# Attention and mixture of experts on one core: every queue in a new order, and twenty filling products instead of thirty

## The chip, the cores and the metric

The kernel runs on one core of one Trainium2 chip, in one launch. The metric is the time of the launch on the device, in microseconds (us); lower is better. Of the engines of a core the kernel uses TensorE (PE in the profile; its weight loads are listed as PEld), VectorE (DVE), ScalarE (ACT), GpSimd (POOL) and SyncE (SP), which only issues transfers.

## What is computed

Eight batches, eight heads, 576 positions, head size 64. The first half computes masked attention per head: heads 0 to 3 see the last 32 positions (local), heads 4 to 7 see every 32nd position (strided). The second half feeds the 512 wide result to four experts, each a causal attention of its own, weighted by a gate that keeps two of four experts per position.

```
scores = scale * q @ k.T;  mask_local = 0 <= rel < 32;  mask_strided = rel >= 0 and same residue mod 32
x = softmax(where(mask, scores, -1e9)) @ v            # (B, S, 512)
logits = x @ w_gate;  w = softmax over the two largest of four
for e in range(4):
    qe, ke, ve = x @ wq[e], x @ wk[e], x @ wv[e]
    a = softmax(where(causal, scale * qe @ ke.T, -1e9))
    out += (e is kept) * w * (a @ ve @ wo[e])
```

## The kernel before

The whole program is written as 2655 small pieces of work ("ops"), collected in a list `OPS`: each has a kind, a batch, the engines that may run it, the buffers that it reads and writes and a function that emits its instructions. Nothing in the code that collects them sets the order. The order is written out in `PLAN`, a table of words: a word such as `63P340` means op 63, on TensorE (P; A is ScalarE, D VectorE, G GpSimd, S SyncE), and the digits behind it give the buffer of a ring that each new tile of the op takes, of eight banks of PSUM for instance. `schedule()` walks through the table and emits each op on the engine that the word names. So the table sets the order on each engine, who evicts a bank, which queue issues a load, and which bank or buffer a tile lies in.

The ops of a batch, with the lines that the profile shows: loads of q and k (L519, L522 for the first heads, L560 later) and of v (L581, L587, L594), most on SyncE, a few on ScalarE and GpSimd; transposes of q and k on TensorE (L539) for the first heads and on VectorE (L571) later; for the first two batches a product that puts the mask into the bank (L643, from `m_loc` or `m_str`); scores of the first attention (L613, L625 local, L632 strided; 72 or 44 products, each of a few rows); row maximum, subtraction, exponential, sum, reciprocal and scaling (L667 to L705; maximum and sums on VectorE, exponential on ScalarE); value products (L757, L777 local, L800 strided; 76, 84 or 44 small products); then x in two parts, `xh` and `xl` (L321, L743). From x the second half takes projections (L944 in batch 0, L933 later; 12 products of 288 columns for half a tile), values (L854, L862), scores (L1035, L987), transposes of the attention weights (L1100, into tiles `th`, evicted in L321), products with V (L1133; 12 or 20) and the output (L1168; 6 products of 512 columns).

The kind `fill` is one product of 448 columns of ones (L336) into a bank that nobody reads; there are `NF` of them, and the table says where they stand. `warm` is eight more of 328 columns at the very start.

```python
        for word in PLAN.split():
            i = 0
            while word[i].isdigit():
                i += 1
            o, slots = OPS[int(word[:i])], iter(word[i + 1:])
            for u in o.uses:
                if not u.taken:
                    u.ring.take(u, int(next(slots)))
            o.fn(ENGINE[word[i]])
    def spin(i):
        wb = RB.new(f"spin{i}")
        op("fill", "P", 448, 0, lambda e: ones(wb, 448), r=[fz], w=[wb], mode=M128)
```

Of the kernel before, what the change touches and what calls it, by code (L numbers as in the profile page):

```python
# [20 lines left out]
def attention_moe_kernel(  # L21
# [72 lines left out]
    NF = 30  # L94
    batch = [0]

    def op(kind, eng, n, key, fn, r=(), w=(), mode=None, npk=0, after=()):
# [26 lines left out]
        17G0123 56S0 4D0 14D01 0D0 10D00 5G 57S 2P01234567 95S0 16D01 3G0 6A 7A 59S 18G0 58A 21A1 92A0 22A 8A  # L124
        96S 9G 24S 15G012 2625P0 71P0 70P1 153P2 91S 23S 93S 2626P3 2627P3 2628P3 2629P3 2630P3 2631P3 2632P3
        63P340 60P56 64A 94S 109P7 65A 61D 35P3 62A 36P4 135S1 72P0 138S1 74D0 134S 73D 76D 139S 75D 78A 136S
        77A 2633P5 2634P5 2635P5 2636P5 2637P5 2638P5 2639P5 2640P5 2641P5 25P561 79D 137S 28P01 27A 26D 29A
        222S0 30D 80D 2642P6 100P650 97P01 224S 81D 102A 37P1 98D 99A 83G 221S 101D 82G 110P5 38D1 223S 111P0
        104G0 39D 41D 236P0 67S1 40D 43A 143P161 112D2 107G 140P43 69S 144A 113D 141A 142D 66S 152P1 145A 114D
        105G 68S 235P3 42A 84D0 154P1 116A 34S2 45D 225P470 115D 106G 201S0 155D3 228P65 227A 44D 226A 32S 230A  # L130
        229D 117A 118D 103G 31S 2643P7 2644P7 237P0 156D 33S 46D 119D 85P7400 47G 192S0 158D 120D 160A 157D 122G
        189S 48D 159A 121D 108G 177S1 49D1 2645P5 2646P5 2647P5 2648P5 123P560 146S1 161D 125A 50P2111 149G 162D
        124A 86A 239D0 180S 88A 163D 87D 193A0 53A 165D 126P6522 195S2 164G 51A 89D 178A0 54D 148G 198S 190A 52D
        191D0 2649P7 2650P7 2651P7 166P741 289S0 238D 1222P10 167A 90G 241D 151S 150G 131A 1260P21 194D 196A
        179D0 1216P7 181A 240D 1261P 183S3 132D 1202P0 242A 147G 182D 1253P3 293S1 127D 129A 168A 1217P 199A
        128D 1209P5 290S 243D 197G 1210P 202S 1223P 130D 12G0 184A 292S 1254P 185D 133G 1262P 338G2 208S1
        169P4633 186S 291S 1218P 174A 172D 200G 244D 203A0 287S 1255P 175D 1A 11G 173D 1211P 170D 212S 1246P6
        13D0 19D0 401S2 171D 1224P 245D 1247P 187A 209S 1248P 188G 295D1 234S0 1203P 288S 20G012345 1204P 213A
        1256P 205S 204G0 1205P 254S1 1225P 210A 214G 1207D0 1263P 286S 1266P4 55G 1264D 324S3 1212P 1226D 1219P
        206A 331S4 211D 1214A 1267P 207G 246D0 1213A 329S 1268P 1206D 397S1 1269P 1228D0 1249P 1208G 328S 1270D  # L140
        1229P50 1250A 294D 253S 176G 1257A 1215G 1251A1 233S 1220A 1258A 336G 303P0 326S 302P6 1230D 304P0 1221D
        325S 1265D1 1305P350 330S 305D1 296G1 306D 327S 1275P7200 307D 255S 1307D0 1237P6 1252G 256S 308D 1276D1
        334G 309A 402S 1280D 1231P5 1306D 337S 1271A 1277D 1308A 1281D 297G 339S 310D 1235P0 1282A 469S0 1272D
        1309A 311D 299S 333D0 312G 1238A 1233P7 1236A 1283A 232S 332D 1227A 218S2 1259G 1232A 1279A 1239P3 362S4
        1273P2401 1234A 1240A 368S3 1242D00 260P601 1241G000 1284P151 1366D2 1243A 364S 1278A 1310D 1361P731
# [1049 lines left out]
    for b in range(B):  # L1195
# [50 lines left out]
```

## Time and profile before

| | |
|---|---|
| median of 3 runs | 447.31 us (447.0 to 447.91) |
| the profiled execution | 443.71 us |
| its span, first to last instruction | 442.0 us |
| TensorE busy | 424.8 us (96%) |
| VectorE busy | 344.0 us (78%) |
| GpSimd busy | 247.8 us (56%) |
| ScalarE busy | 245.9 us (56%) |

A profile shows one execution, here one of 443.71 us. Busy times are the union of an engine's instructions. Products on TensorE overlap, several of them being in the array at once, so a product's own duration is longer than what it adds to the path; what a group adds is read from the start of the group to the start of the next, or from the chain of waits. The chain that ended last runs through TensorE for 81% of the span.

### The profile page before, as it was taken

What the parts mean: (1) busy time and instruction counts of PE and PEld (TensorE: products, weight loads), DVE (VectorE), ACT (ScalarE), POOL (GpSimd) and SP (SyncE); (2) the same over time, 40 slices, a digit from 0 to 9 for tenths busy, and PEclk for the clock granted to TensorE, in tenths of its full rate; (3) what the DMA queues carried; (4) which work ended last, traced back from release to release, by engine and by line L of the source; (5) the groups of instructions that cost most, each with busy time, mean ns of one, the idle gap of its engine ahead of it and who ended that gap; (6) DMA issues with size and microseconds to landing.
All of it is one profiled execution on the core that took longest, in us unless ns stands there. A gap on an engine that the chain in (4) does not pass through costs nothing.

```text
span 442.0 us, 18545 instructions
## 1 busy us (share of the span) xinstructions
PE 424.8 (96%) x7504; PEld 370.3 (84%) x7504; DVE 344.0 (78%) x1043; ACT 245.9 (56%) x759; POOL 247.8 (56%) x439
## 2 busy tenths in 40 slices
PE   7989998999999998999999998999999999999996
PEld 3669977898889976899888897988989998997875
DVE  1797998889999697987798768988787966464833
ACT  3544497425674676634866522852876455557640
POOL 3487776446657357365548441856468522665800
PEclk9999999999999999999999999999999999999999
DMA  8768765664466454644054654557130210003024
GB/s 169 156 138 156 146 129 112 110 111 80 73 135 137 83 94 100 122 92 90 14 104 98 124 104 85 120 114 158 27 73 10 75 49 27 1 2 120 18 82 142
DMA packets 190899, 41.76 MB, mean 94 GB/s; under 512 B 185552, under 2 KB 185808, under 8 KB 190814
## 3 DMA queue, kind: packets, MB, share of 16 engines
q1 hardware_dynamic: 187550, 39.25, 42.6%
q8 instruction: 59, 0.97, 0.9%
q0 software_dynamic: 960, 0.76, 0.8%
q10 hardware_dynamic: 2304, 0.57, 0.6%
q14 instruction: 26, 0.21, 0.2%
HBM read 31.11 MB, written 9.44 MB: 92 GB/s over the span
## 4 chain that ended last, share of the span: by engine, by line
PE 81%; DVE 6%; DMA 3%; SPq 3%; issue 3%; ACT 2%; ACTq 0%; DVEq 0%
PE bank L933 17%; PE bank L1133 10%; PE bank L1168 10%; PE bank L854 9%; PE bank L1035 6%; PE bank L1100 6%; PE bank L800 3%; PE bank L777 3%; PE bank L944 3%; PE bank L625 2%; PE bank L632 2%; PE bank L987 2%; PE bank L862 2%; DVE qkt L571 2%; PE bank L336 2%
## 5 line engine op out<-in xcount | busy, mean ns | idle before, releaser
L1081 POOL TENSOR_SCALAR p<-p,st,wt 128x128 f32<-128x128 f32 (+3 forms) x128 | 77.0, 615 | 20.5 <-DVE st L1061 11.8
L1053 ACT ACTIVATE p<-p,st 128x512 f32<-128x512 f32 (+3 forms) x128 | 72.0, 567 | 8.9 <-DVE st L1048 8.8
L1048 DVE CUSTOM_DVE_ANT_0 p<-bank,m_cau 128x512 f32<-128x512 f32 (+3 forms) x128 | 57.5, 480 | 5.3 <-PE bank L1035 4.1
L571 DVE STREAM_TRANSPOSE qkt<-nat 128x576 f32<-128x576 f32 x52 | 53.0, 1026 | 8.2 <-DMA nat<-in_k_dram 4.3
L321 ACT COPY th<-bank 128x256 f32<-128x256 f32 (+2 forms) x119 | 44.9, 437 | 12.7 <-PE bank L1100 11.9
L1133 PE MATMUL bank<-th,vs 128*64 128x192 f32 (+4 forms) x512 | 48.0, 337 | 0.0
L1133 PEld LDWEIGHTS bank<-th,vs 128*64 128x64 f32 x512 | 33.7, 137 | 14.3 <-issue 7.6
L854 PE MATMUL bank<-wh_v,xh 128*128 128x260 f32 x128 | 36.8, 287 | 0.0
L854 PE MATMUL bank<-wh_v,xl 128*128 128x260 f32 x128 | 36.2, 283 | 0.0
L854 PE MATMUL bank<-wl_v,xh 128*128 128x260 f32 x128 | 36.1, 282 | 0.0
L743 DVE TENSOR_TENSOR xl<-bank,xh 128x128 fp32r<-128x128 f32 (+4 forms) x104 | 32.0, 336 | 4.8 <-ACT xh L321 4.6
L321 ACT CAST xh<-bank 128x270 fp32r<-128x270 f32 (+4 forms) x64 | 20.0, 352 | 25.2 <-PE bank L800 12.6
L1100 PE MATMUL bank<-ident,p 64*128 64x64 f32 x800 | 33.9, 227 | 0.1
L962 POOL TENSOR_TENSOR qkl<-kf,qk 128x288 fp32r<-128x288 f32 x32 | 25.6, 805 | 14.8 <-DVE qk L321 6.2
L933 PE MATMUL bank<-xh,wh_q 128*128 128x288 f32 x112 | 33.7, 301 | 0.0
L933 PE MATMUL bank<-xh,wh_k 128*128 128x288 f32 x112 | 33.6, 300 | 0.0
L1100 PEld LDWEIGHTS bank<-ident,p 64*128 64x128 f32 x800 | 29.2, 138 | 4.7 <-issue 1.3
L933 PE MATMUL bank<-xh,wl_k 128*128 128x288 f32 x112 | 33.0, 295 | 0.0
L933 PE MATMUL bank<-xh,wl_q 128*128 128x288 f32 x112 | 33.0, 294 | 0.0
L933 PE MATMUL bank<-xl,wh_k 128*128 128x288 f32 x112 | 33.0, 294 | 0.0
L933 PE MATMUL bank<-xl,wh_q 128*128 128x288 f32 x112 | 33.0, 294 | 0.0
L705 POOL TENSOR_TENSOR p1s<-p1s,st 128x648 f32<-128x648 f32 (+1 forms) x16 | 19.3, 1209 | 21.4 <-DVE st L703 14.5
(179 smaller groups left out, 1260.0 us busy)
## 6 DMA issues: line engine op xcount, KB each, us to landing
out_dram<-ys SPq DMA_DIRECT2D x31, 256.0 KB
nat<-in_q_dram SPq DMA_DIRECT2D x104, 72.0 KB
nat<-in_k_dram SPq DMA_DIRECT2D x104, 72.0 KB
v<-in_v_dram SPq DMA_DIRECT2D x72, 40.0 KB
v<-in_v_dram SPq DMA_DIRECT2D x110, 22.5 KB
v<-in_v_dram SPq DMA_DIRECT2D x52, 27.0 KB
out_dram<-ys SPq DMA_DIRECT2D x10, 128.0 KB
v<-in_v_dram SPq DMA_DIRECT2D x24, 48.0 KB
```

What stands on the lines that cost most here:

```text
L321: (nc.scalar.copy if e == "ACT" else nc.vector.tensor_copy)(dst, src)
L571: nc.vector.transpose(dst, src)
L743: op("xl", "D", n_, key + 0.5, lambda e, s_=s_, x_=x_: nc.vector.tensor_sub(x_(xl.t), s_(xa.t), x_(f(xh.t))), r=[xa, xh[u]], w=[xl[u]])
L854: nc.tensor.matmul(vp.t[:m, :NV], xx.t[:, t0:t0 + m], ww.t[:, kt, :], start=i == 0, stop=i == 11)
L933: nc.tensor.matmul(pj.t[:, :HS], ww.t[:, kt, ep * 128:(ep + 1) * 128], xx.t[:, c], start=i == 0, stop=i == 11)
L1035: nc.tensor.matmul(sp[a].t[:, c0:c0 + nk], x.t[r, 0, q0:q0 + 128], y.t[r, 1, :nk], start=i == 0, stop=i == 2)
L1048: lambda e, sp=sp, p=p, a=a, nk=nk, ci=ci, c0=c0: nc.vector.tensor_tensor_reduce(out=p.t[:, a, :nk], in0=sp[a].t[:, c0:c0 + nk], in1=m_cau ...
L1053: op("exp2", "A", nk, k_ + 1, lambda e, p=p, a=a, ci=ci, nk=nk: nc.scalar.activation(p.t[:, a, :nk], p.t[:, a, :nk], AF.Exp, bias=st.t[:, ...
L1081: lambda e, p=p, a=a, ci=ci, t=t, nk=nk: nc.gpsimd.tensor_scalar(p.t[:, a, :nk], p.t[:, a, :nk], st.t[:, 14 + ci + a:15 + ci + a], wt.t[:, ...
L1100: nc.tensor.transpose(tp[hf].t[:, 64 * c:64 * c + 64], src, f(ident.t[r, r]))
L1133: nc.tensor.matmul(acc.t[o, c0:c0 + cn], vw, th[a].t[:, s0:s0 + cn], start=j == 0, stop=j == idx[-1], skip_group_check=True)
L1168: nc.tensor.matmul(yp.t[:, :w_], xx.t[:, c0:c0 + 128], ww.t[:, ep, c:c + w_], start=i == 0, stop=i == 5)
```

## The change

Two things differ. `NF` goes from 30 to 20, so ten filling products are gone. And the whole table `PLAN` is another one: all ops but the ten are still there, in another order, on partly other engines, in other buffers. Of the ops that may run on more than one engine, evictions of transposed attention weights stood 119 times on ScalarE and 41 times on VectorE and now stand 109 and 51 times; evictions of V 28 and 12 times, now 23 and 17; evictions and casts of x into `xh` 64 and 40 times, now 69 and 35; those of projections 40 and 24 times, now 43 and 21. On TensorE 146 semaphore instructions become 154. GpSimd issues 34 transfers of v instead of 30.

```diff
     OPS = []
-    NF = 30
+    NF = 20
...
     PLAN = """
-        17G0123 56S0 4D0 14D01 0D0 10D00 5G 57S 2P01234567 95S0 16D01 3G0 6A 7A 59S 18G0 58A 21A1 92A0 22A 8A
...
```

Its places, as the order of the instructions shows them (the names are tiles with their numbers; the rows of an engine stand in the order in which it runs them).

ScalarE at the start, before: `m_loc` is the local mask, copied three times; the four transfers are of q and k.

```order
L370 ACT_TABLE_LOAD
L370 CAST m_loc_77<-m_loc_77 32x320 x2
L519 DMA vs_105<-in_k_dram 64x9x64
L519 DMA vs_106<-in_q_dram 64x9x64
L519 DMA p_97<-in_q_dram 64x8x64
L519 DMA vs_106<-in_q_dram 64x9x64
L370 CAST m_loc_77<-m_loc_77 32x320
L321 COPY qkt_112<-bank_67 128x256
```

And now:

```order
L522 DMA ys_82<-in_q_dram 64x2x64
L332 ACT_TABLE_LOAD
L332 ACTIVATE fz_74<-fz_74 128x1
L519 DMA vs_105<-in_k_dram 64x9x64
L519 DMA vs_105<-in_q_dram 64x9x64
L370 CAST m_loc_77<-m_loc_77 32x320
L519 DMA vs_106<-in_k_dram 64x9x64
L370 CAST m_loc_77<-m_loc_77 32x320 x2
L321 COPY qkt_112<-bank_68 128x320
```

One transfer now stands ahead of the table load, two ahead of the first copy and one between the copies.

TensorE behind the first scores (L613), before: nine filling products (L336, a weight load and a product each) follow them, and then the transposes of the second pair of heads (L539 from `vs1`); two of the nine are shown.

```order
L643 MATMUL bank7_71<-m_str0_78,ident0_76 128x324
L643 MATMUL bank3_67<-m_loc0_77,ident0_76 128x320
L643 MATMUL bank4_68<-m_loc0_77,ident0_76 128x256
L613 MATMUL bank1_65<-qkt0_112 32x64 x20
L613 MATMUL bank0_64<-qkt0_112 32x64 x16
L336 LDWEIGHTS fz0_74
L336 MATMUL bank5_69<-fz0_74 128x448
L336 LDWEIGHTS fz0_74
L336 MATMUL bank5_69<-fz0_74 128x448
```

And now:

```order
L539 MATMUL bank6_70<-ident0_76,vs0_105 128x64
L539 MATMUL bank7_71<-ident0_76,vs0_105 128x64
L613 MATMUL bank3_67<-qkt0_112 32x64 x20
L613 MATMUL bank2_66<-qkt0_112 32x64 x16
L539 MATMUL bank4_68<-ident0_76,vs1_106 128x64
L539 MATMUL bank5_69<-ident0_76,vs1_106 128x64
```

The transposes of the second pair follow the first scores directly; the mask products moved ahead of the first transposes or behind these.

TensorE in the middle of the program, before, where the profile has 288 us: scores of a strided pair of heads (L632) and behind them value products of a local pair (L777, the first four of its pieces).

```order
L632 MATMUL bank4_68<-qkt1_113 64x54
L777 MATMUL bank7_71<-pt11_120,v12_116 64x64 x2
L777 MATMUL bank3_67<-pt11_120,v12_116 64x64 x2
L777 MATMUL bank2_66<-pt11_120,v12_116 64x64 x2
L777 MATMUL bank0_64<-pt11_120,v12_116 64x64 x2
```

In front of the same value products stand now (the six rows of L1168 whole, the first four of twelve of L933):

```order
L632 MATMUL bank2_66<-qkt1_113 64x54
L1168 MATMUL bank5_69<-wh_o0_169,oh2_151 128x512
L1168 MATMUL bank5_69<-wh_o0_169,ol2_154 128x512
L1168 MATMUL bank5_69<-wl_o0_170,oh2_151 128x512
L1168 MATMUL bank5_69<-wh_o0_169,oh0_149 128x512
L1168 MATMUL bank5_69<-wh_o0_169,ol0_152 128x512
L1168 MATMUL bank5_69<-wl_o0_170,oh0_149 128x512
L933 MATMUL bank7_71<-xh5_130,wh_q0_165 128x288
L933 MATMUL bank7_71<-xl5_136,wh_q0_165 128x288
L933 MATMUL bank7_71<-xh5_130,wl_q0_166 128x288
L933 MATMUL bank7_71<-xh4_129,wh_q0_165 128x288
```

Six output products (L1168) and twelve projection products (L933) now stand between the two groups of small products.

## Rows read from the trace of the kernel before

**Rows 1.** The page: busy us (share of the span), instructions.

```profile
PE 424.8 (96%) x7504; PEld 370.3 (84%) x7504; DVE 344.0 (78%) x1043; ACT 245.9 (56%) x759; POOL 247.8 (56%) x439
```

**Rows 2.** Waits of TensorE, 40 to 430 us: us in total, times, longest us.

```profile
PE bank L800 <- issue: 1.7, 1, 1.7
PE bank L777 <- issue: 1.5, 2, 1.1
PE bank L625 <- issue: 1.2, 1, 1.2
PE bank L1035 <- issue: 1.0, 1, 1.0
PE bank L757 <- issue: 0.8, 1, 0.8
PE bank L800 <- DVE st L703: 0.5, 1, 0.5
```

**Rows 3.** Windows between resumptions: length, busy us (instructions) per engine, clock, DMA share, GB/s.

```profile
171.04:244.30 73.26, 71.91 (x1396) 63.05 (x1395) 63.06 (x189) 44.33 (x136) 43.50 (x70) 1.00 0.42 84
244.30:270.10 25.80, 24.56 (x379) 22.65 (x380) 18.42 (x58) 11.12 (x37) 9.44 (x15) 1.00 0.64 122
270.10:289.80 19.70, 18.63 (x383) 16.91 (x383) 18.67 (x49) 10.44 (x34) 13.02 (x23) 1.00 0.42 89
```

**Rows 4.** DMA queues: packets, MB, share of 16 engines; q8 is TensorE's instruction queue.

```profile
q8 instruction: 59, 0.97, 0.9%
```

**Rows 5.** Timeline of TensorE: start us, us, line, count [idle before <- releaser].

```profile
166.88 1.79 PE L625 MATMUL bank<-qkt 64*32 64x64 f32 x144
...
266.61 1.55 PE L800 MATMUL bank<-pt,v 54*64 54x54 f32 x88
...
270.13 0.34 PE L625 MATMUL bank<-qkt 64*32 64x64 f32 x13 [1.24 <-issue]
```

**Rows 6.** Windows from a block's first instruction to the resumption, longest and shortest.

```profile
239.82:244.30 4.48, 3.47 (x132) 3.02 (x128) 4.14 (x13) 2.84 (x9) 4.19 (x8) 1.00 0.49 99
266.84:270.10 3.26, 2.06 (x143) 1.86 (x136) 2.43 (x13) 2.05 (x8) 0.17 (x1) 1.00 0.65 155
```

**Rows 7.** Timeline of TensorE at the start.

```profile
5.96 1.12 PE L643 MATMUL bank<-m_loc,ident 128*128 128x256 f32 x2 [1.85 <-ACT m_loc L370]
...
7.16 2.76 PE L336 MATMUL bank<-fz 128*128 128x448 bf16 x7
9.86 0.78 PE L539 MATMUL bank<-ident,vs 64*128 64x64 f32 x18
...
12.53 1.90 PE L336 MATMUL bank<-fz 128*128 128x448 bf16 x9
...
32.82 0.40 PE L944 MATMUL bank<-xh,wh_q 128*128 128x288 f32 x1
```

**Rows 8.** Windows at the start; columns as in rows 3 (third count: VectorE).

```profile
0.00:10.00 10.00, 6.78 (x23) 3.06 (x25) 1.49 (x8) 2.65 (x4) 3.79 (x22) 1.00 0.85 167
10.00:40.00 30.00, 27.48 (x728) 22.18 (x727) 24.95 (x66) 15.91 (x43) 19.39 (x33) 1.00 0.72 150
```

**Rows 9.** The chain of waits in order of time: start us, us, what.

```profile
77.42 1.45 PE bank L1133 x12
...
291.30 1.58 PE bank L933 x12
292.88 1.41 PE bank L1168 x6
```

**Rows 10.** Timeline of ScalarE, its third copy of the mask.

```profile
5.37 0.46 ACT L370 CAST m_loc<-m_loc 32x320 fp32r<-32x320 f32 x1 [2.07 <-DMA vs<-in_q_dram]
```

**Rows 11.** Timeline of GpSimd, ten issues of loads of v.

```profile
18.25 6.33 POOL L594 DMA_DIRECT2D v<-in_v_dram  x10
```

**Rows 12.** Groups of VectorE by shape: busy us, mean ns of one, idle before.

```profile
L321 DVE COPY th<-bank 128x384 f32<-128x384 f32 x19 | 9.9, 547 | 0.5 <-PE bank L1100 0.5
```

**Rows 13.** Window of the stretch from 100 to 125 us; columns as in rows 3.

```profile
100.00:125.00 25.00, 24.85 (x516) 20.21 (x518) 22.13 (x67) 14.55 (x46) 14.10 (x24) 1.00 0.44 85
```

More of the change, by code (lines that the diff above doesn't have):

```diff
@@ L129, in attention_moe_kernel @@
[L129 to L143, printed above, removed]
@@ L279, in attention_moe_kernel @@
[L279 to L282 removed]
+        95A0 12G0 138S1 15D012 0D0 4D0 14G01 17D0123 1A 59A0 56S 5G 2P01234567 57A 58S 3G0 23S1 6A 24A 18G0 22S
@@ new lines, in attention_moe_kernel @@
+        384G 1422P11 1356A 447D 374S 1483D4 1438G 385D0 1403P0 506S 505S 414G 544D0 606S 448D 1416P4 611S1
+        1539D5 1404A 415A 1423D 406S 485D2 386P375122 481S 416D 1417A 486G 1405A 1357A 449D3 610S 1407P4 507S
+        389D 487A 450G 510D1 408S 387A 393D 488D 1439P0 613S 1402G0 1408A 451A 509S 489D 1409D 220G 391D 540S
+        390D 1413D 1420P2 608S 392D 1440D 1348G 441S1 394D 417D 1406G 1441D 442S 1352P473 511D 1421A 418G
+        1457P650 1354A 680S3 1448P1000 1459D1 541S 490G 1458D 1418P2 445S 419D1 681S 452D 443S 1424P7 1419A
@@ new lines, in attention_moe_kernel @@
+        1725P543 798D 1728P36 1568S 1726A 735P701 797D 1729A 924S 771P150 1730A 1806P230 1777A 923S 772A 1727A
+        1707P600 922S 1808D 736A 1861A 1807D 1856A 799D1 773A 1731P133 1810A 1778D 800G 737A 895D0 1809A
+        1795P4701 1708A 1779G 738P3200 1734A 1709D 838G 774P5011 1888D0 743A 826S2 1811D 741A 1732A 1832D
+        1796P67 739A 801A 1815G 961S1 740D 1736P41 1816G 1889D 779A 828S 802D 777A 775A 1817G 860S1 776D 1813G
+        1572P70 803D 1812G 744D 827S 778D 804G 1833D 1735D 1733D 829S 780D 1821P250 1573A 839D1 1862P611 675G
@@ new lines, in attention_moe_kernel @@
+        2417G 2461P1 2418G 2265A 2564A 2266S 2466A 2463P6 2507A 2563A 2468A 2258P52 2554A 2464D 2558A 2462D
+        2498A 2474D01 2473G000 2497D 2267P31 2475A 2259D 2502A 2506D 2508A 2349P711 2268D 2499A 2557D 2269S
+        2555A 2476D 2405P600 2260S 2350A 2263S 2477G 2503A 2351D 2559A 2509D 2420P100 2406A 2565D 2512G
+        2370P5421 2422A 2426P323 2407D 2513G 2421A 2367P70 2372D 2428A 2566G 2493P1601 2368A 2371D 2515G 2427A
+        2494P24 2530D2 2369A 2569G 2586D3 2364P75 2423P30 2531D 2511G 2366A 2525P161 2424D 2532A 2510G 2425D
@@ L283, in attention_moe_kernel @@
+        2545D 2538A 2542A 2602P2 2544D 2539D 2541D 2546P5 2603A 2605A 2606D 2604D 2607P12 2549A 2547A 2550D
+        2548D 2622P40 2608D 2609S 2613P31 2623D 2624S 2616P72 2614D 2610P00 2617D 2615S 2618S 2270P61 2611D
+        2612S 2619P2 2271D 2620D 2272S 2621S
     """
```

283 lines of the change are left out of this document (140 added, 143 removed).

## The prediction, made before the change was run

> **What bounds the kernel now.** I read the page first. TensorE is busy 424.8 of 442.0 us [rows 1], so the reader should take TensorE's queue as the path and ask only where it stands still. The wait view of TensorE from 40 to 430 us answers that: five waits "issue" of 1.7, 1.5, 1.2, 1.0 and 0.8 us, 6.2 us in all, and behind them one of 0.5 us for VectorE [rows 2]. "Issue" means that no semaphore and no engine held it. What, then?
>
> They stand at regular places. Between the moments at which TensorE goes on again after four of them, the windows count 1396 and 1395 products and weight loads, then 379 and 380, then 383 and 383 [rows 3]: 2791, 759 and 766 instructions, just under 2816, 768 and 768, which are 11, 3 and 3 times 256. The few that lack are semaphore instructions, which the view does not count. The instruction queue of TensorE moved 59 packets and 0.97 MB, 16 KB each [rows 4], one for 256 instructions. So each stall is TensorE reaching the end of a block of 256 whose successor has not landed. It happens where a block is eaten fast: at 266 us two groups of 44 small value products (88 in 1.55 us) and a group of score products stand in a row, and TensorE stops 59 products into it [rows 5]. From the block's first instruction to the moment work resumes took 3.26 us in the shortest of the five cases and 4.48 us in the longest [rows 6]; the other three were 4.26, 3.67 and 3.45 us (mean 3.82). That is my price: a block eaten in less than about 3.8 us leaves the difference as a stall.
>
> The Trainium skill ("Runtime: NRT & Kernel Launch", section "Instruction fetch mechanics") says the same of the block of 256, but also that fetching is mostly hidden, because the sequencer hands out instructions more slowly than blocks arrive. Five waits here speak against the last part [rows 2]; by it they would have another cause and a new order would save none of the 6.2 us. That is rival one.
>
> Before 40 us the picture is another. TensorE is kept busy by filling products: seven in 2.76 us from 7.16 us, nine in 1.90 us from 12.53 us, and more later, 27 in the order before the first projection product, which runs at 32.82 us [rows 7]. They compute nothing. VectorE, which does the row maxima, subtractions and sums of the first scores, is busy 24.95 of 30 us from 10 to 40 us [rows 8], so 5.05 us of it are idle.
>
> **The change, part by part.** *Blocks.* No product but ten fillers goes away, and the order of each kind's work is nearly the old one; what changes is what stands beside what. I counted the new order of TensorE in steps of 256, semaphore instructions included, from the same starting point, and summed each block from rows: 72 score products are half of 1.79 us, 44 value products half of 1.55 us [rows 5], twelve projection products 1.58 us, six output products 1.41 us, twelve products with V 1.45 us [rows 9]. In the old order five blocks after 40 us come out at 3.3, 1.8, 3.1, 2.1 and 2.1 us, and these are the five that stall; no other is under 3.7. At 288 us, for instance, six output and twelve projection products now stand between the score group and the value group: 1.41 + 1.58 = 3.0 us of cover where there was none. In the new order the fast blocks are: one with 88 value and 32 score products and four output products, 1.55 + 0.4 + 0.94 = 2.9 us; one with 72 score, 44 value and six projection products, 0.9 + 0.78 + 0.79 + 0.1 = 2.6 us; one with 112 score products and 16 with V, 1.4 + 1.7 = 3.1 us; one of about 3.4 and one of 3.6 us, mixed. Against 3.82 us they leave 0.9 + 1.2 + 0.7 + 0.4 + 0.2 = 3.4 us of stall. Saved: 6.2 - 3.4 = 2.8 us. By the shortest price, 3.26 us, 0.4 + 0.7 + 0.2 = 1.3 us remain and 4.9 us are saved; by the longest, 4.48 us, 1.6 + 1.9 + 1.4 + 1.1 + 0.9 = 6.9 us, a loss of 0.7 us. I take the mean, since the same sum over the old order (0.5 + 2.0 + 0.7 + 1.7 + 1.7 = 6.6 us) gives the 6.2 us that were seen. All of it lies on the path, since TensorE is the path there and its longest wait for another engine is 0.5 us [rows 2].
>
> *The start.* ScalarE makes three copies of the local mask. The third begins at 5.37 us, when the last of four transfers that it issues itself lets it go, and TensorE's first mask product, at 5.96 us, waits for it [rows 7, 10]. In the new order the same pieces stand ahead (the table, four issues, three copies), but two copies instead of one follow the last issue, so the mask is ready 0.46 us later, not earlier: the first mask product comes at about 6.4 us. Behind it stand two fillers instead of seven (-5 x 0.39 = -2.0 us) and one mask product more (about +0.4 us, a third of the 1.2 us that three take), so the first transposes stand at 9.86 + 0.5 + 0.4 - 2.0 = 8.8 us if their loads have landed; I allow 0.5 us for late loads: 9.3 us, a gain of 0.5 us. Then the nine fillers between the first scores and the second transposes are gone: 1.90 us. The second scores so reach VectorE 0.5 + 1.9 = 2.4 us earlier. VectorE can use this: it had 5.05 us idle. From there both orders run at VectorE's pace into the projections, so I take -2.4 us. Bounds: +0.5 us if everything waits for the later mask; -4.0 us if VectorE's idle time goes down to its one wait of about 1 us for the first scores.
>
> Issues on GpSimd's queue move too: V loads of two pairs of heads now stand among the splits of weights there. Ten such issues took 6.33 us [rows 11]; twelve now stand between the first split and the second, 7.6 us. The projections that need the second split stand behind the last value products in the new order, so I cost it at nothing; with that cover gone it is up to 1 us, inside the bounds above.
>
> *VectorE's share.* Ten evictions of transposed attention weights go from ScalarE to VectorE (119 to 109, 41 to 51), ten smaller pieces of work come with them, eleven go the other way. At 0.55 us for the widest of the ten [rows 12] and 0.4 us for the balance of the rest, VectorE gets 10 x 0.55 - 0.4 = 5.1 us more at most. In the stretch that had 22.13 of 25 us [rows 13] about 3 us are added, so it stands at 25 of 25. It has slack before and behind; I cost it at nothing, and at 5.1 us if the slack cannot be used.
>
> **The sum.** -2.8 (blocks) - 2.4 (start) = -5.2 us. The profiled execution took 443.7 us (span 442.0 and 1.7 around it) and becomes 438.5; the median of the runs shown, 447.3, lies 3.6 above it and becomes 442.1 us. By the bounds: from -8.9 us (438.4) to +0.7 + 0.5 + 5.1 = +6.3 us (453.6).
>
> **The rivals.** *One: the stalls stay.* Either the waits are not the fetch's, or the new fast blocks stall as long as the old. For it: the longest price gives 6.9 us, and the new order still has five blocks under 3.7 us. Against: the multiples of 256. Only the start is gained: 447.3 - 2.4 = 444.9 us.
>
> *Two: the start gives nothing.* The fillers hide waits for loads or for VectorE, so taking them away opens idle time of the same length. A mechanism for that is the clock: the first seven fillers took 0.39 us each and the nine later 0.21 us [rows 7], twice as long and so at the lower of the two levels (1.2 against 2.4 GHz); the granted clock reads 1.00 from 0 to 10 us as it does after [rows 8], so the fillers' own time is the evidence; with fewer fillers TensorE may do its first transposes and scores at the lower one. The skill says so too ("TensorE: Matmul & The Clock Gate", "What's actually happening"): the slow state is the default, and activity ends it. Two us of work at half speed cost 2 us and eat the gain: 447.3 - 2.8 = 444.5 us.
>
> *Three, slower: VectorE becomes the bound.* Place: about 100 us, where it was busy 22.13 of 25 us [rows 13]. If TensorE, rid of its stalls, runs into evictions that wait their turn on VectorE, the block gain is swallowed and up to 5.1 us are added: 447.3 - 2.4 + 5.1 = 450.0 us. It decides once TensorE's waits for VectorE from 40 to 430 us come to over 5 us; the longest now is 0.5 us [rows 2].
>
> **How the numbers follow.** Forecast 0.55, rival one 0.16, two 0.13, three 0.16. The forecast's own range, by the prices, is 438.4 to 445.5 us. The whole range takes in rivals one and two and leaves out the far half of rival three: 438.2 to 447.0 us. A measurement can tell about 0.2%, 0.9 us, from no change. Faster than that: nearly all of the forecast (0.53) and most of rivals one and two (0.22), 0.75; within it 0.11; slower 0.14, nearly all of it rival three.
>
> **What would show it.** In the profile after: TensorE's "issue" waits from 40 to 430 us at 3.4 us or less, each a whole number of 256 instructions from the next, and in blocks with many score and value products; its waits for VectorE still around half a us each at most. First transposes at about 9.3 us, second scores 2.4 us earlier than before, first projection product well before 32.8 us with the same work behind it. It is wrong if the stalls stand in blocks that I summed to over 4 us, if the fillers' place is idle, or if waits for VectorE take over.

## The result, and the profile after

The changed kernel takes 441.55 us (median of 18 runs, 439.09 to 445.87) beside 447.5 us of the kernel before (18 runs). A ratio, here and below, compares the means of those executions that lie within 1.5% of the fastest of their kernel. Here it is 0.9887, with a 95% interval of 0.9857 to 0.9917: 5.1 us or 1.1% faster (3.7 to 6.4 us). The forecast was 5.2 us. The sum was right; two of its terms were not (the stalls saved more, and new waits that it did not have took that back), and they happened to cancel: that was luck.

The profiled execution took 440.58 us, with a span of 438.5 us. The page, busy us (share of the span) and instructions, beside [rows 1]:

```profile
PE 423.2 (96%) x7494; PEld 370.2 (84%) x7494; DVE 348.4 (79%) x1056; ACT 243.4 (55%) x753; POOL 246.7 (56%) x436
```

VectorE has 4.4 us more work, TensorE's share is the same. The waits of TensorE from 40 to 430 us (us in total, times, longest us), beside [rows 2]:

```profile
PE bank L777 <- DMA v<-in_v_dram: 1.3, 1, 1.3
PE bank L625 <- DVE qkt L571: 0.9, 1, 0.9
PE bank L1133 <- ACT p L1053: 0.8, 1, 0.8
PE bank L854 <- DVE qkl L965: 0.5, 1, 0.5
PE bank L800 <- DMA v<-in_v_dram: 0.4, 1, 0.4
```

No "issue" is left: all 6.2 us of [rows 2] are gone. In their place stand waits for operands, 3.9 us in these five rows (four more of 0.2 us follow). The first is for a transfer, and so is the second by way of VectorE, which transposes q and k as they come in (L571, called a turn below). That is what the prediction did not have.

The start, TensorE's timeline beside [rows 7] (start us, us, line, count, [idle before <- releaser]):

```profile
4.72 1.70 PE L643 MATMUL bank<-m_loc,ident 128*128 128x256 f32 x4 [0.46 <-ACT m_loc L370]
6.22 0.97 PE L336 MATMUL bank<-fz 128*128 128x448 bf16 x2
7.12 1.24 PE L539 MATMUL bank<-ident,vs 64*128 64x64 f32 x18
8.80 1.97 PE L613 MATMUL bank<-qkt 64*32 64x64 f32 x72 [0.44 <-ACT qkt L321]
10.70 0.78 PE L539 MATMUL bank<-ident,vs 64*128 64x64 f32 x18
...
12.92 1.21 PE L613 MATMUL bank<-qkt 64*32 64x64 f32 x72
...
25.23 0.44 PE L757 MATMUL bank<-pt,v 32*64 32x64 f32 x11 [1.39 <-issue]
...
27.96 0.40 PE L944 MATMUL bank<-xh,wh_k 128*128 128x288 f32 x1
```

The first transposes stand at 7.12 us instead of 9.86, and there is one wait for a block, 1.39 us, at 25.23 us.

To see where time comes and goes, each group of useful products was given the lower quartile of what its kind took in the trace of before; the work then has a length of 395.8 us in either order, fillers left out. The lag is the start of a group minus the length of what TensorE had done by then. The columns are amounts of work, named by the moment at which the kernel before had done it; names of the experiments are explained below.

| lag of TensorE, us | 40 | 80 | 105 | 170 | 250 | 300 | 400 | end |
|---|---|---|---|---|---|---|---|---|
| before | 18.1 | 21.8 | 23.7 | 27.5 | 35.1 | 38.2 | 41.0 | 42.6 |
| after | 16.0 | 20.5 | 22.7 | 26.1 | 33.2 | 34.7 | 36.5 | 38.2 |
| short fills (before) | 16.9 | 22.2 | 24.4 | 28.1 | 36.8 | 39.8 | 42.7 | 44.3 |
| shift 28 (after) | 14.0 | 17.8 | 20.7 | 27.0 | 36.4 | 37.8 | 39.6 | 41.3 |
| loads earlier (after) | 14.6 | 18.5 | 20.7 | 24.4 | 28.4 | 29.8 | 31.7 | 33.4 |

The change is 2.1 us ahead at 40 us, 1.0 us at 105, 1.9 us at 250 and 4.5 us from 400 on. (0.9 us of that is lost behind TensorE's last product, so the spans differ by 3.5 us.) Since the groups stand in another order, single columns are good to under 1 us only: with groups cut in another way the lead is 0.8 us at 80 us and 1.8 us at 105, and the same within 0.1 us at 40, at 250 and from there on. So about half of the start's gain is gone by 80 or 105 us, and the stalls that go before 250 us (2.7 us from 105 us on) leave about 1 us; only those after 250 us pay in full.

### The profile page after: what moved, and what is told of

It is laid out like the page before. It is cut to its first block, busy times and chain, and to the rows that moved or that the text cites. A ratio compares the mean times of both kernels' runs of the same rounds, so it can differ in the third digit from the quotient of the medians.

```text
span 438.5 us, 18563 instructions
## 1 busy us (share of the span) xinstructions
PE 423.2 (96%) x7494; PEld 370.2 (84%) x7494; DVE 348.4 (79%) x1056; ACT 243.4 (55%) x753; POOL 246.7 (56%) x436
## 4 chain that ended last, share of the span: by engine, by line
PE 75%; DVE 10%; SPq 4%; DMA 4%; issue 2%; ACT 2%; POOL 2%; ACTq 0%; DVEq 0%; POOLq 0%
PE bank L933 17%; PE bank L1168 10%; PE bank L854 9%; PE bank L1133 8%; PE bank L1035 6%; PE bank L1100 5%; PE bank L800 3%; DMA v<-in_v_dram 3%; PE bank L944 2%; DVE qkt L571 2%; SPq L587 2%; SPq L560 2%; DVE p L1048 2%; PE bank L777 2%; PE bank L987 2%
## 5 line engine op out<-in xcount | busy, mean ns | idle before, releaser
L1081 POOL TENSOR_SCALAR p<-p,st,wt 128x512 f32<-128x512 f32 (+3 forms) x128 | 77.0, 614 | 20.2 <-DVE st L1061 15.4
L1053 ACT ACTIVATE p<-p,st 128x384 f32<-128x384 f32 (+3 forms) x128 | 72.0, 566 | 18.7 <-DVE st L1048 18.7
L571 DVE STREAM_TRANSPOSE qkt<-nat 128x576 f32<-128x576 f32 x52 | 52.2, 1023 | 10.0 <-DMA nat<-in_k_dram 7.3
L321 ACT COPY th<-bank 128x384 f32<-128x384 f32 (+2 forms) x109 | 41.8, 434 | 14.5 <-PE bank L1100 12.2
L743 DVE TENSOR_TENSOR xl<-bank,xh 128x270 fp32r<-128x270 f32 (+4 forms) x104 | 32.7, 334 | 5.7 <-ACT xh L321 4.9
L933 PE MATMUL bank<-xh,wh_q 128*128 128x288 f32 x112 | 34.0, 303 | 0.0
L933 PE MATMUL bank<-xh,wh_k 128*128 128x288 f32 x112 | 33.4, 298 | 0.0
L933 PE MATMUL bank<-xl,wh_q 128*128 128x288 f32 x112 | 33.0, 295 | 0.0
L933 PE MATMUL bank<-xh,wl_q 128*128 128x288 f32 x112 | 33.0, 294 | 0.0
L933 PE MATMUL bank<-xh,wl_k 128*128 128x288 f32 x112 | 33.0, 294 | 0.0
L933 PE MATMUL bank<-xl,wh_k 128*128 128x288 f32 x112 | 33.0, 294 | 0.0
L321 ACT CAST xh<-bank 128x270 fp32r<-128x270 f32 (+4 forms) x69 | 21.9, 350 | 18.7 <-PE bank L777 9.2
L321 ACT CAST qk<-bank 128x288 fp32r<-128x288 f32 x43 | 16.9, 403 | 26.2 <-PE bank L933 21.1
```

The costliest lines, as they stand in the source:

```text
L321: (nc.scalar.copy if e == "ACT" else nc.vector.tensor_copy)(dst, src)
L571: nc.vector.transpose(dst, src)
L743: op("xl", "D", n_, key + 0.5, lambda e, s_=s_, x_=x_: nc.vector.tensor_sub(x_(xl.t), s_(xa.t), x_(f(xh.t))), r=[xa, xh[u]], w=[xl[u]])
L933: nc.tensor.matmul(pj.t[:, :HS], ww.t[:, kt, ep * 128:(ep + 1) * 128], xx.t[:, c], start=i == 0, stop=i == 11)
L1053: op("exp2", "A", nk, k_ + 1, lambda e, p=p, a=a, ci=ci, nk=nk: nc.scalar.activation(p.t[:, a, :nk], p.t[:, a, :nk], AF.Exp, bias=st.t[:, ...
L1081: lambda e, p=p, a=a, ci=ci, t=t, nk=nk: nc.gpsimd.tensor_scalar(p.t[:, a, :nk], p.t[:, a, :nk], st.t[:, 14 + ci + a:15 + ci + a], wt.t[:, ...
```

## Experiments

Lines in the first two runs are 3, in the next two 4 below those of the kernel before (L797 is its L800, L621 its L625). Each ratio is to runs of the kernel before on the same chip; the experiments ran on three chips, so runs of different groups are compared by their ratios.

**Moving the block boundaries.** Tiny products behind `warm`, two TensorE instructions each, push every later instruction back; order, operands and loads stay.

```diff
-            ones(x, 328)
+            ones(x, 64)
...
+    def tick(n):
+        wb = RB.new("tick")
...
+            for i in range(n):
+                c = i % 4
+                x = o[64 * (c // 2):64 * (c // 2) + 64, 1:2]
+                nc.tensor.matmul(wb.t[32 * c:32 * c + 32, :16], x.to_broadcast([64, 32]), x.to_broadcast([64, 16]),
...
+    tick(128)
```

> The kernel before, with 128 tiny products (64 by 32 weights, 16 columns, into a bank that nobody reads; each is two TensorE instructions) behind the eight products of warm, and warm's own columns cut from 328 to 64 so that both together fill about the same time. Every later TensorE instruction stands 256 places further back, one whole block: the block boundaries fall on the same products as before. Nothing else changes. Theory F (the waits are the fetch of TensorE's instructions in blocks of 256): the same five waits without a releaser between 40 and 430 us, 1.7, 1.5, 1.2, 1.0 and 0.8 us, 6.2 us in all, in the same places; time as before within 1 us. Theory P (they belong to the products that stand there, to their operands or to the order, whatever the block): the same. So this run only shows what the tiny products themselves cost at the start; it is the yardstick of the next.

Measured: 447.75 us, ratio to before 1.0016 (0.9984 to 1.0048). The waits for a block, 40 to 430 us:

```profile
PE bank L797 <- issue: 1.7, 1, 1.7
PE bank L622 <- issue: 1.5, 2, 1.2
PE bank L754 <- issue: 1.3, 1, 1.3
PE bank L1032 <- issue: 1.0, 1, 1.0
...
PE bank L774 <- issue: 0.9, 2, 0.5
```

The same lines as in [rows 2], 6.4 us. (The tiny products cost 1.9 us at the start of this execution.) The last row holds two waits, 0.49 us at 293.4 us and 0.40 us at 344.8 us. The latter stands at no boundary, as does one of 0.39 us at 340.7 us in the trace of before; so the blocks cost 6.1 us here. With 106 instead of 128 of them:

```diff
-    tick(128)
+    tick(106)
```

> The kernel before, as in the run with 128 tiny products, but with 106 of them: every later TensorE instruction stands 212 places further back, so each block boundary falls 212 instructions earlier in the work (44 later, counted from the next). Order, operands, loads and evictions are those of before. F: by the blocks of before, with the stalls taken out of its times and a price of 3.3 to 3.8 us a block, the waits near 75.6, 169, 243 and 289 us go; near 270 us 0.4 to 0.9 us are left, a new one of 1.4 to 1.9 us stands near 326 us, and up to 0.4 us near 73.5 and 78 us: 1.8 to 3.8 us in all between 40 and 430 us instead of 6.2, and a time 2.4 to 4.4 us below that of the run with 128. P: the five waits stay where they are, 6.2 us, and the time is that of the run with 128.

Measured: 445.31 us, ratio to before 0.994 (0.99 to 0.9979). Against the run with 128 that is 0.76%, 3.4 us less. Executions at the same granted clock (0.999 or above) say the same: 441.55 to 443.03 us (four) beside 445.09 to 447.95 us (three). The trace is of an execution of 449.56 us at a granted clock of 0.989; its stretches at the lower clock, from 100.1 and 199.1 us, touch none of the stalls.

```profile
PE bank L797 <- issue: 0.5, 1, 0.5
PE bank L1130 <- issue: 0.5, 1, 0.5
PE bank L622 <- issue: 0.5, 1, 0.5
PE bank L774 <- issue: 0.4, 1, 0.4
```

1.9 us remain of 6.4 (1.5 us of 6.1 without the wait of 0.4 us, here at 346.5 us, that no boundary explains). The size came out, the places did not: nothing is left near 270 us, the stall of 1.4 to 1.9 us near 326 us did not come, and three of 0.5 us stand at 77.4, 81.9 and 85.9 us. The products, their order and their operands are the same in both; only the boundaries moved. So the stalls belong to the blocks, and rival one's first half (another cause) falls. A count in all fourteen traces says it more sharply: TensorE has 59 waits "issue" over 0.3 us, and 52 of them end where the number of its instructions from the start of the trace leaves the same remainder by 256 (193), whatever the run's shift. The other seven are that one wait of 0.4 us, in the seven runs with the old order. The counter-test, on the changed kernel with 96 tiny products:

```diff
-            ones(x, 328)
+            ones(x, 64)
...
+    tick(96)
```

> The changed kernel with 96 tiny products behind warm (192 TensorE instructions) and warm's columns cut to 64; nothing else changes. F: its order has no wait of this kind after 40 us only because no boundary lies badly. With the boundaries 192 instructions earlier they come back: 1.5 to 2.0 us near 121 us, 1.9 to 2.4 us near 321 us, 0.4 to 0.9 us near 229 us, 0.1 to 0.6 us near 110 us: 4.0 to 6.2 us in all, and a time 3 to 6 us above the changed kernel's 441.5, 444.5 to 447.5 us (up to 0.5 us of it from the start). P: the new order took the cause away, so no such wait comes, and the time stays within 1 us of the changed kernel's.

Measured: 446.08 us, ratio 0.9991 (0.9956 to 1.0026); against the changed kernel's 0.9887 that is 1.04%, 4.7 us more. The stalls are back:

```profile
PE bank L621 <- issue: 1.5, 1, 1.5
...
PE bank L1164 <- DVE p1l L663: 0.9, 1, 0.9
...
PE bank L773 <- issue: 0.4, 1, 0.4
PE bank L753 <- issue: 0.3, 1, 0.3
```

The view puts the second row, at 324.4 us, down to VectorE, but it stands at a boundary, and work resumes 1.3 us after the block's packet has landed, as in the other stalls; I count it with them. It too ends at the remainder of 193. That makes 3.1 us, not 4.0 to 6.2: the place near 229 us that was expected to stall did not, and the one near 321 us took 0.9 us instead of 1.9 to 2.4. A fixed price for a block is too crude; the steps below say why. Of the 4.7 us of time, 3.1 us are these, 0.5 us is a longer wait for the mask at the start (1.0 for 0.5 us), and up to 0.9 us the granted clock (mean of the timed runs 0.996 beside 0.998; an estimate, the difference times the span).

**A stall that costs nothing.** 14 tiny products move the boundary of the one stall that the changed kernel has at 25 us (warm as it was).

```diff
+    tick(14)
```

> The changed kernel with 14 tiny products behind warm (28 TensorE instructions). F: by its blocks none after 40 us is under 3.4 us, so no wait of this kind there, as in the changed kernel; the wait of 1.4 us at 25.2 us, in the block that ran from 20.1 to 23.6 us, goes or shrinks to 0.3 us at most, since that block's boundaries move. Time 0.5 to 1.4 us below the changed kernel's 441.5 us, 440.1 to 441.0 us. P: the wait at 25 us stays and the time is the changed kernel's within 0.4 us, or above it by what the tiny products cost (0.4 us at most).

Measured: 443.03 us, ratio 0.9894 (0.9846 to 0.9942), the changed kernel's within the measurement. Yet the stall is gone (no wait "issue" in the whole trace), and by the table TensorE is 2.0 us ahead of the changed kernel up to 105 us and behind it afterwards. What happened there, in VectorE's and TensorE's timelines, first in the changed kernel, then in this one:

```profile
105.38 0.78 DVE L571 STREAM_TRANSPOSE qkt<-nat 128x576 f32<-128x576 f32 x1 [1.50 <-DMA nat<-in_k_dram]
```

```profile
105.58 0.78 DVE L567 STREAM_TRANSPOSE qkt<-nat 128x576 f32<-128x576 f32 x1 [4.00 <-DMA nat<-in_k_dram]
```

```profile
106.87 0.30 PE L621 MATMUL bank<-qkt 64*32 64x64 f32 x2 [1.99 <-DVE st L1044]
```

A turn of k waits for its transfer and runs at 105.4 or 105.6 us. TensorE arrives 2 us earlier and waits 1.99 us. The transfer is late because SyncE issues it late: in its queue it stands behind others that are needed later. That is not the whole of it. At 94.3 us SyncE too was 2.0 us ahead of the changed kernel. It lost that in two issues of 1.95 and 1.82 us, where the changed kernel's took 0.4 and 0.5 us; in SyncE's timeline, three issues of k each, first in the changed kernel, then in this one:

```profile
102.27 1.80 SPq L560 DMA_DIRECT2D nat<-in_k_dram  x3
```

```profile
101.35 3.11 SPq L556 DMA_DIRECT2D nat<-in_k_dram  x3
```

Each of the two long issues overlaps a packet of TensorE's instructions (at 96.6 and 102.3 us; the last section has the count over all traces). So where the block boundaries lie also shifts the loads. Theory F was right on the stall and wrong on the time; a new theory L (late loads give gains back) takes over.

**The start alone.** Fourteen of the kernel before's fillers made tiny, their number kept, so no boundary moves.

```diff
     for i in range(NF):
-        spin(i)
+        tick(1) if i in (3, 4, 5, 6, 7, 8, 9, 10, 11, 12, 13, 14, 15, 16) else spin(i)
```

> The kernel before with 14 of its filling products made tiny (64 by 32 weights, 16 columns instead of 448): five of the seven ahead of the first transposes, and the nine between the first scores and the second transposes, the ones that the change leaves out. Their number, and so every block boundary, stays. Theory S (my forecast of the start): the first transposes come up to 1.5 us earlier than 9.86 us, the second scores 2.4 to 3.4 us earlier than 16.47 us, and the whole is 2.4 us shorter: 444.9 to 445.1 us beside 447.3 of before. Rival two (the fillers hide waits, or the clock is granted later without them): TensorE idles or runs at the lower level in their place, second scores less than 1 us earlier, time within 0.5 us of before. Theory L (a third one, from the trace of the changed kernel with its boundaries moved by 28: VectorE's turn of a k load at 105.4 us waits 4.0 us for that transfer, whenever TensorE comes): the second scores come 2.4 us or more earlier, but a load's turn on VectorE takes it back by 110 us; time within 0.8 us of before.

Measured: 445.5 us (before beside it: median 446.9), ratio 1.0013 (0.9977 to 1.0049): no gain. TensorE's timeline:

```profile
8.23 1.22 PE L539 MATMUL bank<-ident,vs 64*128 64x64 f32 x18
...
12.91 0.85 PE L539 MATMUL bank<-ident,vs 64*128 64x64 f32 x8 [0.63 <-DVE p1l L688]
...
15.51 1.21 PE L613 MATMUL bank<-qkt 64*32 64x64 f32 x72
...
31.61 0.40 PE L944 MATMUL bank<-xh,wh_q 128*128 128x288 f32 x1
```

The first transposes come 1.6 us earlier, as expected, the second scores only 1.0 us (15.51 for 16.47): in the place of the nine fillers of 1.90 us stands mostly waiting, 0.63 us of it for a bank that VectorE frees. The first projection product is 1.2 us earlier, and by the table the 1.2 us are lost between 40 and 80 us. VectorE there:

```profile
67.34 0.78 DVE L571 STREAM_TRANSPOSE qkt<-nat 128x576 f32<-128x576 f32 x1 [1.22 <-DMA nat<-in_q_dram]
```

Again a turn that waits for a load, 1.22 us; before ran the same turn at 67.28 us without a wait, so VectorE's lead is gone there. The timed runs also show a lower granted clock (mean 0.992, before 0.995: up to 1.2 us). Theory L in its time, rival two in part.

**ScalarE's issues.** The run above with the four issues ahead of the mask copies.

```diff
-6A 7A 59S 18G0 58A 21A1 92A0 22A 8A
+58A 21A1 92A0 22A 6A 7A 59S 18G0 8A
```

> As the run with 14 filling products made tiny, and ScalarE issues its four transfers ahead of the first two mask copies instead of between the second and the third. S: the third copy, and with it TensorE's first mask product (5.96 us before), comes at about 4.7 us, 1.2 us earlier, and the loads of q and k that ScalarE issues land up to 1.5 us earlier; second scores 3.5 to 4.5 us earlier than 16.47 us; time 0.5 to 1.2 us below the run with tiny fillers alone. Had the step of my forecast been right that took the end of the last issue as fixed, the mask product would not move (5.9 to 6.4 us). Rival two: time within 0.5 us of before. L: start earlier by as much, time within 0.8 us of before.

Measured: 448.59 us, ratio 1.0059 (1.0023 to 1.0095): slower, where a gain was expected. ScalarE's timeline, in this run and then in the changed kernel:

```profile
3.61 1.28 ACT L370 ACT_TABLE_LOAD   x1 [3.61 <-issue]
4.90 1.39 ACT L370 CAST m_loc<-m_loc 32x320 fp32r<-32x320 f32 x3
```

```profile
0.80 0.72 ACTq L522 DMA_DIRECT2D ys<-in_q_dram  x1
1.55 1.28 ACT L332 ACT_TABLE_LOAD   x1 [1.55 <-PEq L1230]
...
3.06 1.52 ACT L370 CAST m_loc<-m_loc 32x320 fp32r<-32x320 f32 x3
```

With all four issues first, the table that the copies need loads at 3.61 us and the mask comes at 6.43 us, 0.5 us later. In the changed kernel the tiny exponential (`early`) stands behind the first issue, so the table loads under the other three, and the copies start at 3.06 us. By these rows not the issues' place, but the table's, brings the mask 1.2 us earlier; no run moves the table alone. The loss of 2.6 us is another matter: the mean granted clock of the timed runs is 0.989, beside 0.995 in before, which comes to up to 2.7 us.

**VectorE's share.** Ten of the evictions that the change gives to VectorE, alone; two of the ten words:

```diff
-1492A 1498A
+1492D 1498D
```

> The kernel before with ten of its evictions of transposed attention weights (256 to 384 columns, batches 1 to 3, between about 70 and 210 us) moved from ScalarE to VectorE; the order of every engine's other work stays. It adds about 4.5 us of work to VectorE in a stretch where it was busy 22 of 25 us. Theory of the forecast: the slack hides it, time within 1 us of before. Rival three (VectorE becomes the bound near 100 us): TensorE's waits for VectorE grow by 3 us or more and the time by 2 to 5 us, 449 to 452 us.

Measured: 447.74 us, ratio 1.0037 (1.0002 to 1.0071), 1.7 us for some 4.5 us of work. TensorE's waits for VectorE, 40 to 430 us:

```profile
PE bank L1168 <- DVE ys L321: 1.4, 1, 1.4
...
PE bank L933 <- DVE th L321: 0.5, 1, 0.5
```

Neither nothing nor the rival's 2 to 5 us: the slack hides most of it. Only the second row lies in the stretch of the ten, at 144.4 us. The first stands at 297.8 us, behind two turns in which VectorE waited 2.9 and 0.7 us for loads. So the trace shows 0.5 us for the evictions, and where the rest of the 1.7 us comes from stays open.

**Loads by need.** SyncE's words of the table, near the load of k that was late at 105 us (509), one of 27 such moves on the kernel with 14 tiny products:

```diff
-506S 505S 606S 611S1 406S 481S 610S 507S 408S 613S 509S 540S 608S
+506S 606S 611S1 406S 509S 481S 610S 507S 408S 613S 540S 608S
```

> The changed kernel with 14 tiny products behind warm (28 TensorE instructions), and SyncE's queue reordered in 27 places: a load of q, k or v that landed less than 2.2 us ahead of its use in that kernel's trace is issued one to five places (1 to 4 us) earlier, ahead of loads that are needed later. Nothing else moves. Theory L (late loads give back what TensorE gains: k at 75 and at 105 us, v at 191 us, q and k at 244 us): VectorE's waits for transfers, 11.3 us in all from 40 to 440 us in the run that moved the boundaries by 28, fall under 6 us; TensorE's waits of 2.0 us (local scores at 105 us), 1.5 us (product with V at 78 us) and 1.0 us (local value products at 191 us) go or halve; time 2 to 4 us below that run's 443.0 us median, 439 to 441 us. Rival (SyncE issues back to back there, so that an earlier load makes another late, or VectorE's own work is the bound): the waits move to other places, and the time stays within 1 us of that run.

Measured: 440.11 us, ratio 0.9865 (0.9812 to 0.9918), 1.3 us below the run with 14 tiny products (0.9894), within both intervals: not decided. VectorE's wait at 105 us is down to 0.6 us, but it still waited 8.2 us for loads (the largest row first), the longest time here, with TensorE behind it:

```profile
DVE qkt L571 <- DMA nat<-in_q_dram: 5.0, 4, 2.1
```

```profile
243.70 0.78 DVE L571 STREAM_TRANSPOSE qkt<-nat 128x576 f32<-128x576 f32 x1 [2.13 <-DMA nat<-in_q_dram]
```

```profile
244.62 0.96 PE L625 MATMUL bank<-qkt 64*32 64x64 f32 x72 [1.85 <-DVE qkt L571]
```

So the moves were made larger, by the slack seen in this trace: 52 more.

```diff
-506S 606S 611S1 406S 509S 481S 610S 507S 408S 613S 540S 608S
+506S 509S 507S 606S 611S1 406S 408S 540S 541S 481S 610S 613S 608S
```

> The changed kernel with 14 tiny products behind warm and the loads of the run before it in their new order, and 52 more such moves on SyncE's queue: each load of q, k or v that was issued less than 4.5 us (plus 1.7 us for its way) ahead of its use in that run goes one to seven places earlier, past loads that are needed later. Nothing else moves. Theory L: VectorE's waits for transfers, 8.2 us from 40 to 440 us in that run besides a store's, fall under 4 us; TensorE's 1.9 us of waiting for a turned q at 244 us and 1.3 us for v at 191 us go or halve; time 1 to 3 us below that run's 440.1 us. Rival (the queue issues back to back up to 110 us and the transfers themselves are late, or VectorE is the bound): waits for transfers stay over 6 us, time within 1 us of 440.1.

Measured: 434.94 us, ratio 0.9754 (0.9713 to 0.9795): 2.5% faster than the kernel before and, by the ratios, 1.3% faster than the changed one. VectorE's waits for loads, 40 to 440 us, and TensorE's longest wait from 40 to 430 us:

```profile
DVE qkt L571 <- DMA nat<-in_k_dram: 2.0, 1, 2.0
```

```profile
PE bank L1133 <- DVE xl L743: 1.0, 1, 1.0
```

8.2 us fell to 2.0 us, and the time by 5.2 us (1.1% by the ratios), more than expected. No product, eviction or engine changed; only the order of loads in one queue. The same on the kernel before with short fillers, 50 moves, for instance:

```diff
-266S 264S 434S4 301S 470S3 396S 435S 400S
+265S0 263S 266S 301S 264S 396S 400S 403S 468S 434S4
```

> The kernel before with the 14 filling products made tiny, as in the run of that name, whose start was 1.2 us earlier at the first projection and whose whole was no shorter; now 50 loads of q, k and v that were issued less than 4.5 us (plus 1.7 us for their way) ahead of their use there go earlier on SyncE's queue, past loads that are needed later. Products, fillers and block boundaries stay. Theory L (late loads took the start's gain back between 70 and 110 us): now it stays: time 1 to 3 us below that run's 445.5 us and below before. Rival (the gain was lost to something else, the clock or VectorE): time within 0.8 us of that run's and of before.

Measured: 443.67 us, ratio 0.9938 (0.9904 to 0.9972), 0.75% or 3.4 us below the run with the short fillers alone; the granted clock is the same in both (mean 0.992). The waits "issue" still come to 6.3 us, and no other wait of TensorE from 40 to 430 us is longer than 0.3 us. So the order of the loads is worth 3.4 us on this kernel too. That the loads had held back the start's 1.2 us is not shown. In this trace the start's lead never arose: the clock fell to its lower level for a stretch of the start, and the first projection product came 0.7 us later than in before (windows as in [rows 3]):

```profile
15.82:19.23 3.41, 3.41 (x90) 2.97 (x88) 2.86 (x8) 1.24 (x2) 2.25 (x4) 0.50 0.87 198
```

```profile
33.49 0.40 PE L944 MATMUL bank<-xh,wh_q 128*128 128x288 f32 x1
```

The run with the issues first has such a stretch at 15.5 us too, the one with short fillers alone has none, and none of the other traces has one between 15 and 30 us. So short fillers can cost clock, as rival two said. The missing run is the kernel before with its fillers whole and only the loads moved.

Without the tiny products, with all 79 moves of loads:

```diff
-    tick(14)
```

> The changed kernel with all the moves on SyncE's queue of the run with 52 more of them, but without the tiny products: its block boundaries are those of the changed kernel, with the wait of 1.4 us for the next block at 25.2 us. Theory L: with the loads out of the way the early wait now costs what it lasts: 0.8 to 1.6 us above the run with the tiny products, and 1 to 3 us below the changed kernel's 441.5 us. Rival (SyncE's order is worth nothing, the block's wait too): both equal the changed kernel within 1 us.

Measured, with the changed kernel's own boundaries: 437.64 us, ratio 0.9798 (0.9751 to 0.9844), 2.0 us above the run with the tiny products, where the intervals still touch, and 3.9 us below the changed kernel. The direction is L's: a stall at 25 us that was free (the run with a shift of 28) would cost something once the loads come early. But it isn't shown: in this execution the block waits of the start were 1.3 us in two pieces, the run with the tiny products had one of 0.6 us itself, and a wait of 2.0 us for GpSimd stood at 130 us, as long as the whole difference.

With the tiny products and the loads, and ten evictions back on ScalarE:

```diff
-1492D 1498D
+1492A 1498A
```

> As the run with 52 more moves on SyncE's queue, and ten evictions of transposed attention weights (256 to 384 columns, batches 1 to 3, the ten that were moved to VectorE in the kernel before in an earlier run) go back from VectorE to ScalarE, which takes about 4.5 us of work off VectorE between 70 and 210 us. If VectorE's share costs what it did in the old order (1.6 us for 4.5 us): 0.5 to 1.6 us below the run without this edit. If VectorE has slack once the loads come early: within 0.5 us of it. If ScalarE is late instead: above it, with TensorE's waits for ScalarE growing by 1 us or more.

Measured: 435.54 us, ratio 0.9781 (0.9734 to 0.9827), the same as without the edit (0.9754) within the intervals. The gain of 0.5 to 1.6 us that it should bring if VectorE's share still cost something isn't seen, which fits slack for the ten evictions once the loads come early; the intervals are too wide to exclude 0.5 us.

## Why the prediction came out, step by step

*What bounds the kernel: half right.* TensorE's queue, and the five stalls as the fetch of blocks of 256 instructions: shown by the two shifts of the kernel before (6.4 and 1.9 us of stall, 3.4 us of time), by the stalls that a shift brought into the new order, and by the count. (The row of 1.5 us in [rows 2] is two waits, 1.07 us at 289.8 us and 0.39 us at 340.7 us. The second stands at no boundary, so blocks are 5.8 of the 6.2 us; what it waits for stays open.) The Trainium skill ("Runtime: NRT & Kernel Launch", "Instruction fetch mechanics") calls fetching mostly hidden; the kernel before shows 5.8 us of 442 that were not. The step that failed is the question asked of the waits: only TensorE's were read. VectorE's waits for loads, 8.1 us from 40 to 440 us in the trace of before (8.9 after), were left out. These are the largest rows of before; beside the stalls they limit the launch, since moving loads alone gave 3.4 us on the short fillers with the stalls in place, and 6.3 us on the new order without them:

```profile
DVE qkt L571 <- DMA nat<-in_k_dram: 4.3, 4, 2.0
DVE qkt L571 <- DMA nat<-in_q_dram: 3.4, 2, 2.1
```

*Blocks: right in kind, wrong in size.* Predicted 3.4 us left, 2.8 us saved; measured none left, 6.2 us saved (5.8 of them blocks), outside the step's own bounds (0.7 us lost to 4.9 us saved). The term that failed is the price of 3.82 us per block, taken as a constant. In 53 stalls over 0.3 us in thirteen traces, work resumes 1.2 to 1.6 us after the block's packet on TensorE's instruction queue has landed, and the packet takes 0.9 to 1.6 us; that much is fixed. But it starts anywhere from 0.2 us before to 3.5 us after TensorE's first instruction of the block that it is eating. In the five stalls of before [rows 2], two of them in [rows 6], it happened to start late, 0.8 to 1.9 us after. The trace of before already had the counterexample, against "no other is under 3.7": the block from 366.4 to 369.7 us was eaten in 3.3 us without a wait, its successor's packet having started 1.3 us before its first instruction. The changed kernel's five fastest blocks after 40 us, 2.8, 2.9, 3.1, 3.5 and 3.5 us long, had their packets start 0.4 us after, 0.5 us after, 0.6 us before, 1.2 us after and 0.3 us before: ready in time. Ahead of them stand projections and output products of 0.1 to 0.2 us each, so that the sequencer may have run ahead; that this is the reason is argued, not shown. (In the working, 16 products with V at 1.45 us for twelve are 1.9 us, not 1.7; that block sums to 3.3 us.)

*The start: -2.4 us predicted, -2.1 us at 40 us, by another way, and about half of it gone by 105 us.* The mask step failed: I held the end of the last issue at 5.37 us [rows 10], and the mask came at 4.72 us, not 6.4, since the table load had moved under the issues. The first transposes so came at 7.12 (9.3 predicted), the second scores 3.5 us earlier (2.4 predicted); a stall of 1.39 us at 25 us and waits for ScalarE and VectorE took 1.4 us back by 40 us. The assumption that nine fillers' 1.90 us are all gain failed too: with them short, 1.0 us of 3.5 us arrived at the second scores.

*GpSimd's issues: nothing, as costed.* TensorE's longest wait for GpSimd after 40 us is 0.2 us. *VectorE: nothing predicted, up to 1.7 us measured* for the ten evictions in the old order (0.5 us of it seen in the trace), none seen with early loads.

*The sum.* -2.8 and -2.4 make -5.2; it was -6.2 for the stalls, -2.1 for the start and +3.7 for operand waits (4.7 us after 40 us where before had 1.0), together -4.6; TensorE's own difference by the table is -4.4, that of the two spans -3.5. The timed difference of 5.1 us is larger. The clock can account for that: its mean in the timed runs is 0.998 after and 0.995 in the runs of before beside the experiments, up to 1.3 us of 445, while the two traces stand at 0.998 and 1.000. So the agreement with 5.2 us has a second piece of luck in it.

*The rivals.* One falls, its second half too (the new fast blocks did not stall). Two happened in small: the first transposes and scores took 1.24 and 1.97 us, the second ones 0.78 and 1.21 us, so by their lengths 1.2 us went to the lower level of the clock, and the start was ahead all the same; for short fillers alone, the time of rival two is what was measured, and the granted clock was lower (0.992). Three did not come: TensorE's waits for VectorE after 40 us are 1.8 us, not over 5. Its picture, an engine behind TensorE that takes its gains back near 100 us, was the right one, with the loads as what is late instead of VectorE's work.

## What to carry to other kernels

Before TensorE's waits are priced, look at the engine behind: where it waits 2 us for a load beside a stall of the same length, removing the stall may give nothing. List for each transfer the time from issue to use; an issue queue that is mostly busy (SyncE issued for 60 of 70 us from 40 to 110 us in before) should go in the order of need, and here that alone was worth 1.4%, 6.3 us (0.9894 to 0.9754), beside the 5.1 us of the whole new order. Whether a stall belongs to a block of instructions is shown cheaply: push the program back by a few tiny instructions and see whether the stall moves, or count the instruction at which it ends modulo 256.

## What the runs showed of the hardware

A wait of TensorE can cost twice. In the run with the boundaries moved by 28, the windows before, after and behind the wait at 104.9 us (length, busy us of PE, PEld, DVE, ACT, POOL, clock, DMA share, GB/s):

```profile
103.49:106.87 3.38, 1.39 (x14) 1.30 (x12) 1.29 (x4) 0.76 (x2) 0.71 (x1) 1.00 0.47 78
107.08:110.49 3.41, 3.23 (x80) 1.98 (x80) 3.41 (x13) 0.49 (x2) 1.23 (x1) 0.50 0.58 104
110.49:115.00 4.51, 4.51 (x132) 3.65 (x130) 4.08 (x17) 2.40 (x9) 0.05 (x1) 1.00 0.50 94
```

After 1.99 us of waiting the granted clock is 0.50, the lower level (1.2 of 2.4 GHz), from 107.08 to 110.49 us; the group of twelve products with V takes 2.42 us there and 1.52 us at full clock in the changed kernel:

```profile
108.62 2.42 PE L1129 MATMUL bank<-th,vs 128*64 128x384 f32 x12
```

```profile
108.03 1.52 PE L1133 MATMUL bank<-th,vs 128*64 128x384 f32 x12
```

Over the fourteen traces there are twelve such stretches between 15 and 430 us. Ten began 0.2 to 1.5 us after a wait of TensorE of 0.8 to 2.0 us; the two at the start, with short fillers, began 0.3 and 0.8 us after two waits of 0.6 and 0.4 us. But of 37 waits of 1 us or more there, only nine were followed by one within 2 us.

A fetch of TensorE's instructions goes with a slow issue on SyncE. From 40 to 430 us of the fourteen traces SyncE issued 6977 transfers. Of these, 367 took over 1.0 us (median 1.4 us, the others 0.4 us), and every one of the 367 overlaps a packet on TensorE's instruction queue; about half of the 744 packets there have such an issue beside them. That is about 26 issues in each trace, which together take some 25 us more than at 0.4 us each. What issue and fetch share is not shown.
